# Attention, experts and a gated MLP on one core: the cap with the first keys, reciprocals spread over partitions, signs and copies on ScalarE

## The chip, the cores and the metric

The kernel runs on one core of a Trainium2 chip. The metric is the device time of one execution in microseconds. The core has TensorE (PE in the profile; PEld is its weight load), VectorE (DVE), ScalarE (ACT), GpSimd (POOL), and SyncE (SP), which here only issues transfers.

## The reference

Three blocks in a row, all in float32, for batch 4, sequence 448, 12 heads of 64.

```python
scores = cap * np.tanh(scale * (q @ k.T) / cap)     # per batch and head
attn = np.exp(scores - scores.max(-1, keepdims=True))
x = attn / (attn.sum(-1, keepdims=True) + 1e-09) @ v    # heads side by side: [4, 448, 768]

logits = x @ w_gate                                 # 4 experts, the 2 best are weighted
for e in range(4):                                  # causal attention, head size 64
    ye = softmax(causal(x @ wq[e] @ (x @ wk[e]).T / 8)) @ (x @ wv[e]) @ wo[e]
    out += gate(logits, e) * ye

h = gelu(out @ w_in)                                # 768 -> 1024
u, v = h[..., :512], h[..., 512:]
v = layer_norm(v) * g_ln
y = out + (u * (w_sg @ v + b_sg[:, None])) @ w_out
```

`w_in` and `w_out` arrive as float64 and are turned into float32 on the chip, by integer operations on their upper and lower words.

## The kernel before, in words

The first block runs in 25 slots (`slot`), one for each pair of heads and one to finish: 4 batches x 6 pairs. Transposed keys and queries lie in `kp` and `qp` (two heads on 128 partitions, 448 columns). In slot i TensorE makes the scores of pair i (`scores`), three and a half blocks of 128 keys for two heads; ACT takes tanh (scale `tsc`, 1/(8 cap)) and then exp (scale `capt`) into `p`, a ring of four buffers; TensorE multiplies pair i-1 with its values (`values`) into `po`, which ACT copies to `os`. DVE (and POOL from batch 1 on) adds the blocks of exp up (`add_up`, tile `pb`), and in every second slot a product with ones (`sums`) turns two pairs' `pb` into sums over the keys. They gather in one tile `rs` a batch, in which 32 partitions belong to each of four heads and only three of the 32 hold sums that are needed.

`invert` ends a batch: DVE takes the reciprocal of the whole tile `rs`, SP stores it to DRAM (`rd`), and `load_rb` reads it back, broadcast over 64 partitions (`rb`). Two slots later `over_sums` multiplies `os` by `rb`, and `in_parts` splits the result into `xh` and `xl`, from which the second block's products read.

A slot has places at which side work is called: `a` twice (written a0 and a1), `w`, `p`, `n`. In slots 0 to 9 the side work is `prepare_weights`: twelve units of `w_in` are loaded, turned into float32 (`convert`, which calls `from64`, seven DVE operations on 128x512) and multiplied with `wo` on TensorE (`products`, a slot or two after their unit). The list `turns` says which units a slot converts: one in slots 0, 1, 2, 4, 6, 8, two in 3, 5, 7. From slot 10 on the side work is the second block for batches 0 to 2 (`PLAN`): projections (`queries_keys`, `values_chunk`), softmax (`weigh`, `settle`), transposes of the probabilities (`turn`, tile `pt`), products with values (`attend`). `values_chunk` also yields the gate's logits in the last four columns of its PSUM tile; ACT copies the values to `vp`, DVE the logits to `lg`. `normed` calls `invert`, `load_rb`, `over_sums` and `in_parts` of batch b at fixed places of the next batch: `invert` at a1 of its second slot (7, 13, 19), `over_sums` at `w` of its fourth.

Until the end of slot 24, ACT, DVE, POOL and TensorE keep the order in which the program calls them; SP's issues are placed by the planner. After slot 24 the rest of the second block (`experts_end`) and the third block (`mlp_a`, `mlp_b`, `mlp_c`) run together, and the planner orders all engines.

Of the kernel before, what the change touches and what calls it, by code (L numbers as in the profile page):

```python
# [74 lines left out]
def build(ctx: ExitStack, tc: tile.TileContext, a: dict):  # L75
# [68 lines left out]

    def scale():
        nc.sync.dma_start(capt, a["cap"].to_broadcast([128, 1]))
        dve.memset(tsc, 0.0)
        act.activation(tsc, tsc, AF.Tanh)
        dve.reciprocal(tsc, capt)
        dve.tensor_scalar(tsc, tsc, 1.0 / math.sqrt(D), None, op0=ALU.mult)  # L150
# [7 lines left out]

    def from64(w, m, e):


        words = w.bitcast(I32).rearrange("p (n t) -> p n t", t=2)
        up, down = words[:, :, 1], words[:, :, 0].bitcast(U32)
        f, ef = m.bitcast(F32), e.bitcast(F32)
        dve.tensor_scalar(m, up, 0x7FFFFFFF, None, op0=ALU.bitwise_and)
        dve.tensor_scalar(f, f, LO64, HI64, op0=ALU.max, op1=ALU.min)
        dve.tensor_scalar(m, m, 3, 0x3FFFFFF8, op0=ALU.logical_shift_left, op1=ALU.bitwise_and)
        dve.scalar_tensor_tensor(m, up, -0x40000000, m, op0=ALU.bitwise_and, op1=ALU.bitwise_or)
        dve.tensor_scalar(e, m, -0x800000, None, op0=ALU.bitwise_and)
        dve.scalar_tensor_tensor(ef, down, 2.0 ** -52, ef, op0=ALU.mult, op1=ALU.mult)  # L170
        return f, ef
# [6 lines left out]
    ps_o = ah.enter_context(tc.tile_pool(name="ps_o", bufs=1, space=PSUM, side="right"))  # L178
    os_t, sums_t, pend, rb_d = {}, {}, {}, {}
    vt, ptail, po_t = {}, {}, {}  # L180
# [10 lines left out]
    def load_pair(b, hp):  # L191

        qp = at.tile([128, S], F32, tag="qp", name=f"qp{b}_{hp}", bufs=3)
        kp = at.tile([128, S], F32, tag="kp", name=f"kp{b}_{hp}", bufs=3)
        nc.sync.dma_start(kp, a["kT"][b, :, hp, :])
        nc.sync.dma_start(qp, a["qT"][b, :, hp, :])
        if (b, hp) == pairs[0]:
            scale()
            load_w(0)
        return qp, kp, load_v(b, hp)  # L200

# [6 lines left out]
    def tails(s, *of):  # L208
# [3 lines left out]
        for w, (qp, kp) in enumerate(of):  # L212
            for j in range(2):
                r = slice(64 * j, 64 * j + 64)
                mm(s[64 * w:64 * w + 64, j, :S], kp[r, KB * 128:], qp[r, :], start=True, stop=True)

# [61 lines left out]
    def sums(b, i):  # L278
# [4 lines left out]
        if i == 0:  # L283
            sums_t[b] = ao.tile([128, S], F32, name=f"rs{b}", tag="rs", bufs=1)
            dve.tensor_copy(sums_t[b], g[:, :S])
        else:
# [3 lines left out]
    def invert(b):  # L290
        dve.reciprocal(sums_t[b], sums_t[b])
        d = dr.tile([4, 32, S], F32, tag="rd", name=f"rd{b}")
        nc.sync.dma_start(d.rearrange("j r s -> (j r) s"), sums_t[b])
        rb_d[b] = d
        for h2 in range(2):
            load_rb(b, h2)

# [3 lines left out]
    def slot(i, side):  # L301
# [6 lines left out]
        if i + 2 < len(pairs):  # L308
            qk = [at.tile([128, S], F32, tag=t, name=f"{t}{i + 2}", bufs=3) for t in ("qp", "kp")]
            b, hp = pairs[i + 2]  # L310
            nc.sync.dma_start(qk[1], a["kT"][b, :, hp, :])
            nc.sync.dma_start(qk[0], a["qT"][b, :, hp, :])
            ld[i + 2] = qk
# [17 lines left out]
        if i == len(pairs):  # L331
            drain(sums(B - 1, HP // 2 - 1))
            invert(B - 1)
        side("p")
        if 0 < i < len(pairs):
# [31 lines left out]
    def normed(n, place):  # L367
# [3 lines left out]
        if n >= B * HP or b < 0:  # L371
            return
        if step == (1, "a1"):
            invert(b)
        elif step == (3, "w"):
            over_sums(b, 0)
# [55 lines left out]
    def values_chunk(b, c):  # L432
        xh, xl = X[b]
        if c == 0:
            VP[b] = mo.tile([CP, NC, E * HD], F32, tag="vp", name=f"vp{b}", bufs=2)
            LG[b] = sm.tile([CP, NC, E], F32, tag="lg", name=f"lg{b}")
        g = ps_g.tile([128, 512], F32, tag="g", name=f"v{b}_{c}")
        n = 0
        for k in range(KC):
# [4 lines left out]
            yield 360.0  # L444
        act.activation(VP[b][:, c, :], g[:CP, :E * HD], AF.Copy)
        dve.tensor_copy(LG[b][:, c, :], g[:CP, E * HD:E * HD + E])

    def gates(b):

        lg = LG.pop(b)  # L450
        sh = [CP, NC, E, E]
# [56 lines left out]
    def turn(b, ep, el):  # L508
        pt = PTS[b, ep, el] = mo.tile([CP, NC, S], F32, tag=f"pt{el}", name=f"pt{b}_{ep}_{el}")
        for i in range(NC):  # L510
# [3 lines left out]
            for j in range(i + 1):  # L514
                pin(nc.tensor.transpose(g[:CP, j * CP:(j + 1) * CP], pe[:, j * CP:(j + 1) * CP], ident))  # L515
            rnd("a" if 2 * b + ep >= PTA and i % 2 < PTE else "v", pt[:, :i + 1, i * CP:(i + 1) * CP],
                g[:CP, :n].rearrange("p (j q) -> p j q", q=CP))
# [13 lines left out]

    QKT, VP, LG, WT, CSS, PES, PTS = {}, {}, {}, {}, {}, {}, {}

# [145 lines left out]
    def prepare_weights(pool):  # L679
# [10 lines left out]
        def convert(u):  # L690
            m = pool.tile([128, FH], I32, name=f"wi{u}m", tag="m64", bufs=5)
            e = pool.tile([128, FH], I32, name=f"wi{u}e", tag="e64", bufs=2)
            p, e = from64(raw.pop(u), m, e)
            dve.tensor_tensor(p, p, e, op=ALU.add)
# [276 lines left out]
def _layout(x):  # L971
# [7 lines left out]
        "vt": v[:, :, KB * 128:].reshape(B, HP // 2, 2, 2, KT, D).transpose(0, 1, 2, 4, 3, 5).reshape(B, HP // 2, 2 * KT, 2, D),  # L979
        "cap": np.asarray(x["cap"]).reshape(1, 1),  # L980
        "wqk": _rows(np.concatenate([wide(x["moe_wq"]), wide(x["moe_wk"])], 1)),
# [7 lines left out]
        "b_sg": x["moe2_b_sg"].reshape(1, S),  # L989
    }  # L990
    r = np.arange(CP)
    hot = np.zeros((128, 3, 32), np.float32)
# [27 lines left out]
```

## Time and profile before

| | us |
|---|---|
| median of 3 runs | 552.34 (551.21 to 554.4) |
| profiled execution | 549.69 |
| its span, first to last instruction | 547.9 |
| TensorE busy | 518.1 |
| VectorE busy | 353.4 |
| ScalarE busy | 310.1 |
| GpSimd busy | 130.4 |

The timed runs are whole executions; the profile is one execution of its own. Times inside it count from its first instruction. A busy engine is one with an instruction under way; for TensorE the ends of matmuls are modelled. Line 106 is the helper through which ACT, DVE and POOL instructions go, line 121 that of matmuls and 515 the transposes, so instructions are told apart by the names of their tiles. A name after `<-` in brackets is what ended the idle time before an instruction.

### The profile page before, as it was taken

To read this page: it belongs to the slowest core of one execution; us is meant where nothing else is said; L and a number is where in the kernel's file an instruction comes from. 1 tells how busy PE (TensorE), PEld (TensorE's weight loads), DVE (VectorE), ACT (ScalarE), POOL (GpSimd) and SP (SyncE) were. 2 spreads that over 40 slices of the span, in tenths; PEclk is the share of its full clock that TensorE was granted. 3 is DMA by queue.
4 is the path that set the end of the run, shared out by engine and by line. 5 is a ranking of instruction groups with operands and counts; after the bars stand their busy time and mean duration, and the time that the engine had idled before them with its cause. 6 is when DMAs were issued, how large, how long until landed. Compare 5 with 4: busy or idle time off the path is not lost.

```text
span 547.9 us, 7557 instructions
## 1 busy us (share of the span) xinstructions
PE 518.1 (95%) x2732; PEld 336.9 (61%) x2732; DVE 353.4 (64%) x720; ACT 310.1 (57%) x507; POOL 130.4 (24%) x151
## 2 busy tenths in 40 slices
PE   7999997999999998999997999899899999999997
PEld 2233332355545564554556758669678889889996
DVE  3899999983757745656765678756622796484300
ACT  5978675778685786485743573542544353253211
POOL 0000130433145071135143437304603010010000
PEclk9999997999999999999998999999899999999999
DMA  7964614653334241323025811210511000000111
GB/s 266 346 199 144 199 49 153 205 183 111 100 86 144 60 145 26 117 62 92 1 74 133 216 32 39 65 52 0 210 72 51 1 1 34 34 35 34 51 51 67
DMA packets 33157, 53.99 MB, mean 99 GB/s; under 512 B 4128, under 2 KB 28000, under 8 KB 33120
## 3 DMA queue, kind: packets, MB, share of 16 engines
q1 hardware_dynamic: 31968, 48.27, 28.6%
q0 software_dynamic: 1152, 5.24, 2.9%
q8 instruction: 21, 0.34, 0.3%
q14 instruction: 16, 0.13, 0.1%
HBM read 41.84 MB, written 11.67 MB: 98 GB/s over the span
## 4 chain that ended last, share of the span: by engine, by line
PE 58%; DVE 24%; ACT 6%; DMA 4%; issue 4%; POOL 3%; SPq 1%; DVEq 0%; POOLq 0%; ACTq 0%
PE o L121 15%; DVE pb L106 7%; PE sp L121 6%; PE qk L121 6%; PE v L121 5%; ACT p L106 4%; PE hv L121 4%; PE s L121 4%; PE po L121 4%; PE hu L121 4%; PE av L121 3%; PE a L121 3%; PE tr L515 2%; DVE rs L106 2%; POOL pe L106 2%
## 5 line engine op out<-in xcount | busy, mean ns | idle before, releaser
L106 ACT ACTIVATE p<-s,tsc 128x896 f32<-128x896 f32 x84 | 80.7, 1005 | 37.0 <-PE s L121 18.7
L121 PE MATMUL s<-qp,kp 64*128 64x448 f32 (+1 forms) x384 | 80.0, 574 | 3.6 <-ACT p L106 3.6
L106 POOL TENSOR_TENSOR pb<-p 128x896 f32<-128x896 f32 x18 | 41.4, 2301 | 162.9 <-ACT p L106 148.1
L106 ACT ACTIVATE p<-p,capt 128x1792 f32<-128x1792 f32 (+1 forms) x48 | 77.0, 1603 | 1.3
L106 DVE TENSOR_TENSOR pb<-pb,p 128x896 f32<-128x896 f32 (+1 forms) x48 | 56.5, 1178 | 11.1 <-ACT p L106 7.4
L121 PE MATMUL po<-p,vv 128*64 128x448 f32 x288 | 59.9, 551 | 0.0
L121 PEld LDWEIGHTS s<-qp,kp 64*128 64x128 f32 (+1 forms) x384 | 27.5, 175 | 49.9 <-issue 22.9
L106 POOL TENSOR_SCALAR pe<-pe,cs 112x112 f32<-112x112 f32 (+1 forms) x64 | 37.1, 600 | 51.8 <-DVE cs L106 50.0
L106 DVE CUSTOM_DVE_ANT_0 a<-a,neg 112x112 f32<-112x112 f32 (+3 forms) x64 | 28.2, 462 | 29.7 <-PE a L121 29.3
L106 ACT ACTIVATE pe<-a,m 112x112 f32<-112x112 f32 (+3 forms) x64 | 31.4, 494 | 25.8 <-DVE m L106 21.2
L121 PEld LDWEIGHTS po<-p,vv 128*64 128x64 f32 x288 | 18.7, 138 | 38.8 <-issue 34.3
L121 PE MATMUL qk<-xh,wqk_h 128*128 128x448 f32 x96 | 37.6, 393 | 1.4 <-DVE xh L106 1.4
L121 PE MATMUL o<-gh,wu_h 128*128 128x448 f32 x96 | 36.3, 378 | 0.2 <-DMA wu_h<-wud 0.2
L121 PE MATMUL o<-gl,wu_h 128*128 128x448 f32 x96 | 36.0, 375 | 0.0
L121 PE MATMUL qk<-xh,wqk_l 128*128 128x448 f32 x96 | 35.4, 368 | 0.0
L515 PE MATMUL tr<-ident,pe 112*112 112x112 f32 x160 | 25.2, 263 | 10.6 <-DVE pt L106 3.7
L121 PE MATMUL o<-gh,wu_l 128*128 128x448 f32 x96 | 34.9, 368 | 0.0
L106 ACT ACTIVATE ob<-o 128x448 f32<-128x448 f32 x24 | 13.0, 542 | 38.6 <-PE o L121 38.1
L106 POOL TENSOR_TENSOR rstd<-rstd,mhalf 112x1 f32<-112x1 f32 x16 | 10.2, 640 | 102.0 <-DVE rstd L106 102.0
L121 PE MATMUL v<-wvg_h,xh 128*112 128x260 f32 x96 | 28.8, 300 | 2.3 <-DVE lg L106 2.2
L515 PEld LDWEIGHTS tr<-ident,pe 112*112 112x112 f32 x160 | 17.8, 133 | 18.6 <-issue 13.4
L121 PE MATMUL a<-qk 64*112 64x112 f32 (+3 forms) x128 | 27.9, 427 | 0.8 <-ACT qk L106 0.6
(227 smaller groups left out, 1111.0 us busy)
## 6 DMA issues: line engine op xcount, KB each, us to landing
kp<-in_kT_dram SPq DMA_DIRECT2D x24, 224.0 KB, 3.7
qp<-in_qT_dram SPq DMA_DIRECT2D x24, 224.0 KB, 3.9
rb<-rd SPq DMA_DIRECT2D x24, 224.0 KB, 5.2
out_dram<-ob SPq DMA_DIRECT2D x24, 224.0 KB, 1.9
vv<-in_v_dram SPq DMA_DIRECT2D x24, 192.0 KB, 3.6
wuw<-in_w_out_dram SPq DMA_DIRECT2D x6, 384.0 KB, 3.5
wud<-wuw SPq DMA_DIRECT2D x12, 192.0 KB, 1.9
ws<-in_wqk_dram SPq DMA_DIRECT2D x4, 384.0 KB, 6.0
```

Of the source, the lines that this page charges most:

```text
L106: ins = f(*args, **kw)
L121: pin(nc.tensor.matmul(*args, **kw))
L515: pin(nc.tensor.transpose(g[:CP, j * CP:(j + 1) * CP], pe[:, j * CP:(j + 1) * CP], ident))
```

## The change

The cap is no longer an input of its own: it is the last column of a copy of the first pair's keys (`k_cap`, 449 columns), loaded in two transfers of 128 and 321 columns; the first queries are issued on ACT's queue. DVE takes the scale's reciprocal from that column and copies it to `capt`. For units 2 to 11, `from64` makes the absolute value of the upper words with an ACT activation (Abs) instead of a DVE mask. The first of each batch's three `sums` is copied from PSUM by ACT. `invert` is split: at a0 the sums are stored to DRAM as they are; at `w` (`spread`) the 3 x 448 sums of each of the four heads are read back as 32 partitions x 42 columns; at a1 (`inverted`) DVE takes the reciprocal of 128x42 and four stores return it; the broadcasts start at `w` of the next slot. For the last batch the steps follow one another. The logits stay in `vp` (four more columns of ACT's copy), and the copies of the transposes of batches 0 and 1 for the second expert of the first pair go from DVE to ACT.

```diff
-    def scale():
-        nc.sync.dma_start(capt, a["cap"].to_broadcast([128, 1]))
+    def scale(with_keys):
         dve.memset(tsc, 0.0)
         act.activation(tsc, tsc, AF.Tanh)
-        dve.reciprocal(tsc, capt)
+        dve.reciprocal(tsc, with_keys)
+        dve.tensor_copy(capt, with_keys)
         dve.tensor_scalar(tsc, tsc, 1.0 / math.sqrt(D), None, op0=ALU.mult)
...
-        dve.tensor_scalar(m, up, 0x7FFFFFFF, None, op0=ALU.bitwise_and)
+        if by is act:
+            act.activation(f, up.bitcast(F32), AF.Abs)
+        else:
+            dve.tensor_scalar(m, up, 0x7FFFFFFF, None, op0=ALU.bitwise_and)
...
-        kp = at.tile([128, S], F32, tag="kp", name=f"kp{b}_{hp}", bufs=3)
-        nc.sync.dma_start(kp, a["kT"][b, :, hp, :])
-        nc.sync.dma_start(qp, a["qT"][b, :, hp, :])
+        kp = at.tile([128, S + 1], F32, tag="kp", name=f"kp{b}_{hp}", bufs=3)
         if (b, hp) == pairs[0]:
-            scale()
+            act.dma_start(qp, a["qT"][b, :, hp, :])
+            for c in (slice(0, 128), slice(128, S + 1)):
+                nc.sync.dma_start(kp[:, c], a["k_cap"][:, c])
+            scale(kp[:, S:])
             load_w(0)
+        else:
+            nc.sync.dma_start(kp[:, :S], a["kT"][b, :, hp, :])
+            nc.sync.dma_start(qp, a["qT"][b, :, hp, :])
...
-            dve.tensor_copy(sums_t[b], g[:, :S])
+            act.activation(sums_t[b], g[:, :S], AF.Copy)
...
     def invert(b):
-        dve.reciprocal(sums_t[b], sums_t[b])
-        d = dr.tile([4, 32, S], F32, tag="rd", name=f"rd{b}")
+        d, n = dr.tile([4, 32, S], F32, tag="rd", name=f"rd{b}"), 3 * S // 32
         nc.sync.dma_start(d.rearrange("j r s -> (j r) s"), sums_t[b])
+        rows = d[:, :3, :].rearrange("j r s -> j (r s)").rearrange("j (p c) -> j p c", c=n)
+        r = ao.tile([128, n], F32, name=f"ri{b}", tag="ri", bufs=1)
+        inv[b] = (r, rows)
         rb_d[b] = d
-        for h2 in range(2):
-            load_rb(b, h2)
+
+    def spread(b):
+        r, rows = inv[b]
+        for j in range(4):
+            nc.sync.dma_start(r[32 * j:32 * j + 32], rows[j])
+
+    def inverted(b):
+        r, rows = inv.pop(b)
+        dve.reciprocal(r, r)
+        for j in range(4):
+            nc.sync.dma_start(rows[j], r[32 * j:32 * j + 32])
...
             invert(B - 1)
+            spread(B - 1)
+            inverted(B - 1)
+            load_rb(B - 1, 0)
+            load_rb(B - 1, 1)
...
-        if step == (1, "a1"):
+        if step == (1, "a0"):
             invert(b)
+        elif step == (1, "w"):
+            spread(b)
+        elif step == (1, "a1"):
+            inverted(b)
+        elif step == (2, "w"):
+            load_rb(b, 0)
+            load_rb(b, 1)
...
-        act.activation(VP[b][:, c, :], g[:CP, :E * HD], AF.Copy)
-        dve.tensor_copy(LG[b][:, c, :], g[:CP, E * HD:E * HD + E])
+        act.activation(VP[b][:, c, :], g[:CP, :E * HD + E], AF.Copy)
...
-        lg = LG.pop(b)
+        lg = VP[b][:, :, E * HD:]
...
-            rnd("a" if 2 * b + ep >= PTA and i % 2 < PTE else "v", pt[:, :i + 1, i * CP:(i + 1) * CP],
+            rnd("a" if 2 * b + ep >= PTA and i % 2 < PTE or (ep, el) == (0, 1) else "v", pt[:, :i + 1, i * CP:(i + 1) * CP],
...
-            p, e = from64(raw.pop(u), m, e)
+            p, e = from64(raw.pop(u), m, e, act if u > 1 else dve)
...
-        "cap": np.asarray(x["cap"]).reshape(1, 1),
...
+    out["k_cap"] = np.concatenate([out["kT"][0, :, 0, :], np.full((2 * D, 1), x["cap"], np.float32)], 1)
```

## Rows read from the trace of the kernel before

**Rows 1.** The page: TensorE's share; DVE and granted clock (tenths) in 40 slices of 13.7 us.

```profile
PE 518.1 (95%) x2732; PEld 336.9 (61%) x2732; DVE 353.4 (64%) x720; ACT 310.1 (57%) x507; POOL 130.4 (24%) x151
...
DVE  3899999983757745656765678756622796484300
...
PEclk9999997999999999999998999999899999999999
```

**Rows 2.** Who waited for whom: us in total, times, longest us.

```profile
PE sum L121 <- DVE pb L106: 3.3, 1, 3.3
...
PE qk L121 <- DVE xh L106: 1.4, 1, 1.4
...
PE tr L515 <- DVE pt L106: 3.7, 3, 1.3
...
PE tr L515 <- DVE lg L106: 1.5, 1, 1.5
...
PE tr L515 <- ACT os L106: 1.0, 1, 1.0
...
PE v L121 <- DVE lg L106: 2.2, 1, 2.2
...
PE o L121 <- DMA wu_h<-wud: 0.2, 1, 0.2
...
ACT p L106 <- DVE pb L106: 13.2, 3, 7.3
```

**Rows 3.** Stretches; columns PE, PEld, DVE, ACT, POOL busy, clock, DMA, GB/s.

```profile
20.00:83.40 63.40, 63.24 (x294) 20.99 (x292) 61.11 (x88) 48.31 (x48) 6.98 (x3) 1.00 0.54 169
...
84.00:87.20 3.20, 0.03 (x2) 0.03 (x3) 3.13 (x4) 0.00 (x0) 0.00 (x0) 0.85 0.26 90
...
87.20:95.00 7.80, 7.80 (x26) 2.33 (x26) 7.56 (x12) 7.72 (x7) 0.00 (x0) 0.62 0.63 185
```

**Rows 4.** Timeline of the start: start us, length us, engine, line, what.

```profile
0.73 1.28 ACT L106 ACT_TABLE_LOAD   x1 [0.73 <-PEq L1009]
...
5.49 1.77 PE L121 MATMUL s<-qp,kp 64*128 64x448 f32 x8
...
7.22 1.91 ACT L106 ACTIVATE p<-s,tsc 128x896 f32<-128x896 f32 x2 [5.00 <-DVE tsc L106]
```

**Rows 5.** Timeline of slots 7 to 9, DVE.

```profile
70.78 0.41 DVE L106 TENSOR_SCALAR wi9m<-wi_3w 128x512 int32<-128x512 int32 x1
...
82.11 2.94 DVE L106 RECIPROCAL rs<-rs 128x448 f32<-128x448 f32 x1
...
95.46 2.08 DVE L106 TENSOR_TENSOR os<-os,rb 128x896 f32<-128x896 f32 x2
```

**Rows 6.** Groups by shape: busy us, mean ns of one, idle us before.

```profile
L106 DVE RECIPROCAL rs<-rs 128x448 f32<-128x448 f32 x4 | 11.8, 2947 | 0.0
...
L106 DVE RECIPROCAL cs<-cs 112x4 f32<-112x4 f32 x16 | 2.8, 176 | 0.5
...
L106 ACT ACTIVATE w2h<-w2ps 128x512 fp32r<-128x512 f32 x4 | 2.4, 598 | 1.9 <-PE w2ps L121 1.9
...
L106 DVE COPY lg<-v 112x4 f32<-112x4 f32 x16 | 2.5, 154 | 16.7 <-ACT vp L106 16.7
```

**Rows 7.** DMA issues: KB each, median us from issue to landing.

```profile
capt<-in_cap_dram SPq DMA_DIRECT2D x1, 0.5 KB, 5.0
...
rd<-rs SPq DMA_DIRECT2D x1, 224.0 KB, 1.9
...
rb<-rd SPq DMA_DIRECT2D x24, 224.0 KB, 5.2
```

**Rows 8.** Timeline of slots 12 and 13, DVE.

```profile
134.69 0.62 DVE L106 TENSOR_TENSOR rs<-rs,sum 128x448 f32<-128x448 f32 x1 [0.36 <-PE sum L121]
...
141.38 2.95 DVE L106 RECIPROCAL rs<-rs 128x448 f32<-128x448 f32 x1
```

**Rows 9.** What SP's queue waited for: us in total, times, longest us.

```profile
SPq L185 <- PE po L121: 68.2, 13, 11.9
```

More of the change, by code (lines that the diff above doesn't have):

```diff
@@ L157, in build, with from64 @@
     w2_d = [dr.tile([128, 2, FF], F32, name=f"w2d{i}", tag="w2d") for i in range(2)]
-    def from64(w, m, e):
+    def from64(w, m, e, by=None):
         words = w.bitcast(I32).rearrange("p (n t) -> p n t", t=2)
@@ L178, in build @@
     ps_o = ah.enter_context(tc.tile_pool(name="ps_o", bufs=1, space=PSUM, side="right"))
-    os_t, sums_t, pend, rb_d = {}, {}, {}, {}
+    os_t, sums_t, pend, rb_d, inv = {}, {}, {}, {}, {}
     vt, ptail, po_t = {}, {}, {}
@@ L214, in tails @@
                 r = slice(64 * j, 64 * j + 64)
-                mm(s[64 * w:64 * w + 64, j, :S], kp[r, KB * 128:], qp[r, :], start=True, stop=True)
+                mm(s[64 * w:64 * w + 64, j, :S], kp[r, KB * 128:S], qp[r, :], start=True, stop=True)
     def scores(b, hp, h, qp, kp, then=None):
@@ L308, in slot @@
         if i + 2 < len(pairs):
-            qk = [at.tile([128, S], F32, tag=t, name=f"{t}{i + 2}", bufs=3) for t in ("qp", "kp")]
+            qk = [at.tile([128, n], F32, tag=t, name=f"{t}{i + 2}", bufs=3) for t, n in (("qp", S), ("kp", S + 1))]
             b, hp = pairs[i + 2]
-            nc.sync.dma_start(qk[1], a["kT"][b, :, hp, :])
+            nc.sync.dma_start(qk[1][:, :S], a["kT"][b, :, hp, :])
             nc.sync.dma_start(qk[0], a["qT"][b, :, hp, :])
@@ L434, in values_chunk @@
         if c == 0:
-            VP[b] = mo.tile([CP, NC, E * HD], F32, tag="vp", name=f"vp{b}", bufs=2)
-            LG[b] = sm.tile([CP, NC, E], F32, tag="lg", name=f"lg{b}")
+            VP[b] = mo.tile([CP, NC, E * HD + E], F32, tag="vp", name=f"vp{b}", bufs=2)
         g = ps_g.tile([128, 512], F32, tag="g", name=f"v{b}_{c}")
@@ L530, in attend @@
         act.activation(YA[b][:, ep, :], g[:, :S], AF.Copy)
-    QKT, VP, LG, WT, CSS, PES, PTS = {}, {}, {}, {}, {}, {}, {}
+    QKT, VP, WT, CSS, PES, PTS = {}, {}, {}, {}, {}, {}
     PLAN = {0: [("p", queries_keys, 0, 0)],
```

## Prediction

> **What bounds the kernel now.** I read the page first. TensorE (PE) is busy for 95% of the span, but in the first seven of forty slices DVE too stands at 8 or 9 tenths, and the granted TensorE clock drops in slices 7, 22 and 29 [rows 1]. So two engines are candidates, in different stages. The second view was what matmuls waited for [rows 2]: TensorE's visible waits are few, and most name DVE. The third was the table of stretches [rows 3]. From 20 to 83.4 us TensorE is busy for 63.2 of 63.4 us, at full clock, although DVE is almost as full (61.1). There DVE's length costs nothing yet. It falls behind, and the bill comes at 84 to 87.2: TensorE does nothing, then runs from 87.2 to 95 at a mean 0.62 of full clock, between its two levels of 1.2 and 2.4 GHz. The timeline [rows 5] shows why: the reciprocal of the first batch's sums holds DVE for 2.94 us until 85.05, and the additions that the next sums need come behind it; ScalarE (ACT) waited for such additions too, 13.2 us in three places, 7.3 in the longest [rows 2]. The reader should see a kernel bound by TensorE, with holes. The change can win the holes and the slow clock behind them, and nothing of what lies between.
>
> The holes: 3.3 us (sums behind additions), 1.4 (first projection behind `xh`), 3.7 (transposes behind DVE copies, three times), 1.5 and 2.2 (behind the copies `lg`), 1.0 (behind ACT's `os`) [rows 2]. The slow clock after the first hole costs 7.8 x 0.38 = 3.0 us [rows 3]. The profiled execution took 549.69 us with a span of 547.9; the median of the three runs, 552.34, is 2.65 above it. I take the difference found in the profile off that median.
>
> **Part 1, the cap with the first keys.** The first tanh began at 7.22, after ACT had idled 5.00 us for the scale, which DVE makes from the cap. The first scores began at 5.49 and half of their 1.77 us serves the first tanh, so without the cap it could begin near 6.5: 0.7 us [rows 4]. It is nothing if the keys, now in two transfers, or the queries, now issued by ACT, land later than 5.5, and 0.8 at most. The added copy of the cap is one short DVE instruction (0.18 for a reciprocal of 4 columns [rows 6]) while DVE idles. The issue on ACT stands in front of a table load that ended at 2.0 [rows 4], three us before it matters. SP has one issue less in front of the first weights.
>
> **Part 2, ten signs to ACT.** Units 2 to 11 lose their first DVE step, 0.41 [rows 5] and its gap, 0.44: 4.4 us. ACT gains ten passes over 128x512; the nearest row is 0.60 [rows 6], so 6.0 us. From 20 to 83.4 ACT is busy 48.3 of 63.4 [rows 3], and nine of the ten come there (5.4): 53.7 still fits. But ACT works in program order, so a sign stands behind its slot's two tanhs and in front of the exp, and DVE can run no further ahead than that. The page "ScalarE: Activation LUTs" of the Trainium skill (section "Table sets: the hidden batching unit") counts abs among the cheap functions that every table set holds. The trace has a single table load, of 1.28 us [rows 4], and no abs, so it cannot show it; were the page wrong, twenty loads would cost 25.7 us. By that rule this gets no chance of its own.
>
> **Part 3, the reciprocal spread out.** 128x448 takes 2.95 and 112x4 takes 0.18 [rows 6]; that is 6.2 ns a column, so 42 columns take about 0.41 and DVE saves 2.5, four times. The price is a longer way: sums to DRAM (1.9 [rows 7]), four loads, the reciprocal, four stores, then the broadcasts. The trace has no such load; the nearest rows are 1.9 (a store of 224 KB) and 5.0 (the cap, 4 bytes a row) [rows 7]. SP spends some 0.4 us on an issue of this kind, 1.5 on four. So the way from ready sums to the reciprocal's inputs is 1.9 + 1.5 + 1.9 = 5.3 us, or 8.4 by the cap's row. I take the lower: with 168 B these rows are 11 times shorter than the store's (1,792 B) but 42 times longer than the cap's. In slot 13 the last sums are ready at 135.3 and the reciprocal stood at 141.38 [rows 8]: 6.1 us, so it just fits. In slot 7 there is more room.
>
> **Part 4, copies and logits to ACT.** DVE loses the first copies of the sums (0.62 like the addition in [rows 8], four times, two of them in the first stage), sixteen `lg` copies of 0.15 with 16.7 us of waiting for ACT in front of them [rows 6], and eight copies of transposes in slots 15 and 21. ACT takes each at less than the 0.60 of its copy of 512 columns [rows 6], and the logits ride in a copy that it made already.
>
> **The sum.** *Start to first projection.* ACT's wait for additions near 62 us goes with the lag, so slot 7's scores can come at 64.8 - 0.7, the first half of them, two tanhs and the sign behind it 0.9 + 1.9 + 0.6 later: 67.5, where DVE began the unit (9) at 70.78. Units 9 and 10 then took until 82.11 [rows 5]; less two signs that is 10.4, and with 0.4 for the reciprocal DVE is at 78.3 and has the additions by 80.5. TensorE wants them at 83.4 - 0.7 = 82.7, so the hole and its slow clock go (3.3 + 3.0). The next limit is `xh`: four stores issued from 78.3, landed at 81.7; four broadcasts issued by 84, 0.6 each, and landed after 5.2 or more [rows 7], say at 90.3; the two products then end at 91.5 where they ended at 97.54 [rows 5], 6.0 earlier, and DVE's work behind them is the same. I take 5.5 for all parts up to here (bounds 2.0, if DVE waits at each sign, and 0.7 + 3.3 + 3.0 + 1.4 = 8.4).
>
> *Slots 10 to 24.* Transposes behind DVE: 3.6 of 3.7, as two places lose the copies and at the third the reciprocal in front of them shrinks. The 1.0 behind `os` goes too: the gates in front of it start later by the reciprocal and `lg`. Behind `lg`, only 0.3 of 1.5, because ACT's own copy ended just before it. Sum 4.9 (bounds 1.5 and 3.7 + 1.0 + 1.5 = 6.2).
>
> *The last batch.* TensorE waited 2.2 us for an `lg` that DVE did after products waiting for broadcasts [rows 2], and the clock of slice 22 stands at 8 tenths [rows 1], 1.4 to 2.7 us of 13.7. With the logits off DVE both can go: +3.7. But the broadcasts come later: 1.9 + 1.5 + 1.9 + 0.4 + 1.5 + 1.9 = 9.1 instead of 2.95 + 1.9, so 4.2 us more, and softmax work queued behind the products on DVE would wait as long. Between +3.7 and -4.2 I take +1.0: the planner is free in its order here and can place the products later, since their projections come much later.
>
> *After 300 us* nothing is removed but `lg`; a new order may win or lose: 0, bounds -2 and +2.
>
> 5.5 + 4.9 + 1.0 = 11.4, and 552.3 - 11.4 = **540.9 us**, the likeliest case's own range 538 to 544.5.
>
> **The rivals.** (a) *ACT sets the pace* (0.17): if each sign delays the exp that TensorE's next products need, 6.0 us return: 547. For it: from 87.2 to 95 ACT is busy 7.7 of 7.8. Against it: 15 us of ACT's idle time from 20 to 83.4 [rows 3].
> (b) *All holes go* (0.13): 8.4 + 6.2 + 3.7 = 18.3, so 534. For it: DVE's savings in the first stage (4.4 + 1.2 + 2.5 + 0.7 = 8.8) exceed its holes. Against it: the broadcasts above.
> (c) *It does not do what it says* (0.07): the signs hold DVE at ACT's pace, the additions still come at 87, and transposes wait for ACT's copies instead of DVE's. The 0.7 at the start and half a us beside it remain: 551.
> (d) *The short loads are slow* (0.06): each takes the cap's 5.0 instead of 1.9. At slots 13 and 19 the reciprocal then waits 8.4 - 6.1 = 2.3 us, and the last batch pays 3.1 twice, for load and store: 540.9 + 4.6 + 6.2 = 551.7. For it: the cap's row is the only one here with short rows. Against it: the cap was queued behind 448 KB of keys and queries. The Trainium skill's page "DMA: Bandwidth & Descriptors" (section "Specifications") speaks for it: it gives 512 B as the least transfer for line rate, and a row of the spread has 168 B. No row here shows that size.
> (e) *Slower* (0.07): SP's order stops DVE. SP takes its issues in turn, and a load of values has waited 11.9 us there for TensorE [rows 9]; loads of the spread queued behind such a one leave DVE standing at the reciprocal, and behind that its transposes, softmax and additions. At slots 13 and 19 and in the last batch it must hold DVE 3.8 us each, beyond the 6.1 that are covered, to eat the 11.4; at 6 us each the time is 559. For it: eight more issues a batch, all waiting on one another. Against it: the one transfer that a matmul visibly waited for cost 0.2 us [rows 2], whatever SP's queue waited.
> My forecast has 0.50. Half a per cent, 2.8 us, is about what a measurement of this kernel can tell from no change. So faster 0.80, same 0.13, slower 0.07. The range 533 to 550 has (a) and most of (b) inside; (e), about half of (c) and (d), and a third of (b) lie outside.
>
> **What would show it.** First tanh near 6.5; no hole near 84 and full clock to 95; the projection's last keys near 104; reciprocals of 0.4 with no DMA as their releaser; no transposes behind DVE in slots 15, 19 and 21; no `lg`. It is wrong if DVE waits for ACT at the clamps or for DMA at the reciprocals, or if a new hole follows the last batch.

## The result and the profile after

The changed kernel takes 545.73 us (median of 4 runs, 545.04 to 546.0) beside 551.86 for the kernel before (4 runs): a ratio of 0.9879, with an interval of 0.9845 to 0.9912. That is 6.1 us less where 11.4 were forecast. The profiled execution took 545.04 with a span of 543.2, 4.7 less than before; the marks and tables up to the experiments are about these 4.7.

The page after: TensorE's share, then DVE and the granted clock in 40 slices (of 13.6 us).

```profile
PE 516.1 (95%) x2732; PEld 336.6 (62%) x2732; DVE 333.2 (61%) x683; ACT 319.0 (59%) x529; POOL 132.2 (24%) x151
...
DVE  3899999874466646456724596755722796484300
...
PEclk9999999999999999999999899799999999999999
```

Against [rows 1] the 7 of slice 7 is gone. The 8s of slices 22 and 29 have given way to an 8 in slice 23 and a 7 in slice 26. VectorE lost 20 us of work and ScalarE won 9, but neither number says where the time went. The waits do (us in total, times, longest):

```profile
PE tr L542 <- POOL pe L106: 4.6, 2, 2.9
...
PE qk L121 <- DVE xh L106: 2.3, 1, 2.3
PE qk L121 <- ACT pe L106: 1.8, 1, 1.8
...
PE tr L542 <- ACT pt L106: 1.2, 2, 0.7
...
PE tr L542 <- DVE pt L106: 0.5, 1, 0.5
...
ACT p L106 <- DVE pb L106: 5.8, 3, 3.1
```

Of [rows 2], the wait of the sums (3.3), the `lg` (1.5 and 2.2), the `os` (1.0) and nearly all of the transposes behind VectorE (3.7) are gone. The list also has waits that [rows 2] do not show. The two longest are transposes behind GpSimd's `pe` and a projection behind ScalarE's `pe`. They lie in the last batch.

To place the gains, take the first matmul of each slot's values product as a mark. Slot 11's mark came 5.36 us earlier (114.50 before, 109.14 after). Of the later slots five are shorter: slot 14 by 1.6, 15 by 0.6, 18 by 1.1, 19 by 1.2, 21 by 0.6. Slot 24, the last, is reached at 266.25 where it was 276.79: 10.54 us ahead, and 11.6 counted from the first scores, which begin 1.05 later in this execution. From there to the last output matmul before took 267.46 and after takes 273.32. So 10.5 were won and 5.9 given back. The two tables of that last part, first before, then after, each in five stretches (columns as in [rows 3]):

```profile
276.79:306.79 30.00, 26.62 (x166) 18.65 (x165) 19.73 (x59) 10.30 (x32) 9.25 (x17) 0.94 0.52 139
306.79:336.79 30.00, 29.29 (x148) 21.44 (x147) 23.36 (x66) 19.73 (x47) 14.89 (x18) 1.00 0.30 80
336.79:371.79 35.00, 32.26 (x176) 24.27 (x174) 22.02 (x56) 16.73 (x42) 10.58 (x16) 1.00 0.15 46
371.79:411.79 40.00, 37.79 (x204) 30.76 (x203) 21.03 (x64) 16.39 (x43) 15.24 (x26) 0.96 0.27 97
411.79:544.25 132.46, 132.45 (x654) 118.17 (x652) 64.14 (x119) 47.37 (x90) 8.79 (x14) 1.00 0.10 35
```

```profile
266.25:296.25 30.00, 27.45 (x176) 19.11 (x175) 11.97 (x37) 9.49 (x30) 8.66 (x15) 1.00 0.60 167
296.25:326.25 30.00, 24.74 (x115) 16.73 (x114) 23.53 (x66) 18.22 (x45) 14.16 (x15) 0.94 0.16 44
326.25:361.25 35.00, 32.26 (x155) 26.00 (x154) 23.70 (x64) 16.29 (x42) 13.65 (x18) 0.90 0.17 54
361.25:401.25 40.00, 37.54 (x217) 30.85 (x216) 21.57 (x60) 16.16 (x43) 14.50 (x24) 1.00 0.22 79
401.25:539.57 138.32, 138.32 (x682) 121.13 (x681) 66.80 (x129) 50.00 (x96) 9.95 (x16) 1.00 0.11 39
```

TensorE's idle time is the stretch less its busy time: 9.05 in sum before, 13.01 after, 4.0 more. The second stretch alone has 4.6 more. The clock's price is the length times what is missing to 1.00: 3.4 before, 5.3 after, 1.9 more. The remainder is 255.0 in both, so what was given back is idle time and the slow clock behind it. (The clock column has two digits, so its price is good to about 0.2 us.) The table of experiments below uses the same two numbers.

Why TensorE idles there is seen on VectorE, after, in the last batch:

```profile
271.33 0.62 DVE L106 TENSOR_TENSOR rs<-rs,sum 128x448 f32<-128x448 f32 x1 [0.29 <-PE sum L121]
276.93 0.42 DVE L106 RECIPROCAL ri<-ri 128x42 f32<-128x42 f32 x1 [4.97 <-DMA ri<-rd]
...
280.05 0.56 DVE L106 SCALAR_TENSOR_TENSOR wum<-wuw,wum 128x384 f32<-128x384 uint32 x1
285.29 1.09 DVE L106 TENSOR_TENSOR os<-os,rb 128x896 f32<-128x896 f32 x1 [4.68 <-DMA rb<-rd]
286.30 0.63 DVE L106 CUSTOM_DVE_ANT_0 a<-a,neg 112x448 f32<-112x448 f32 x1
...
288.30 1.09 DVE L106 TENSOR_TENSOR os<-os,rb 128x896 f32<-128x896 f32 x1 [1.32 <-DMA rb<-rd]
...
296.15 1.09 DVE L106 TENSOR_TENSOR os<-os,rb 128x896 f32<-128x896 f32 x1 [5.92 <-DMA rb<-rd]
```

and the same two kinds of line in the kernel before:

```profile
292.92 1.09 DVE L106 TENSOR_TENSOR os<-os,rb 128x896 f32<-128x896 f32 x1 [2.15 <-DMA rb<-rd]
...
294.77 1.09 DVE L106 TENSOR_TENSOR os<-os,rb 128x896 f32<-128x896 f32 x1 [0.29 <-DMA rb<-rd]
...
296.17 0.56 DVE L106 SCALAR_TENSOR_TENSOR wum<-wuw,wum 128x384 f32<-128x384 uint32 x1
299.31 1.21 DVE L106 TENSOR_TENSOR os<-os,rb 128x896 f32<-128x896 f32 x1 [1.91 <-DMA rb<-rd]
```

Three products with broadcasts wait 4.3 us before and 11.9 after; counted from slot 24's mark the third stands at 22.5 before and at 29.9 after. The step `wum`, the end of a weight conversion, stands behind two of the products before and ahead of all three after. The order in this part is the planner's. GpSimd waits for that step, and then sends for 2 MB of `w2`, before and after (start us, length, engine, what):

```profile
296.87 0.52 POOL L106 TENSOR_SCALAR wuw<-wum 128x384 fp32r<-128x384 f32 x1 [13.11 <-DMA rb<-rd]
...
299.52 1.29 POOL L796 DMA_DIRECT2D w_h<-w2d  x2
```

```profile
280.76 0.51 POOL L106 TENSOR_SCALAR wuw<-wum 128x384 fp32r<-128x384 f32 x1 [7.55 <-issue]
...
283.38 1.29 POOL L823 DMA_DIRECT2D w_h<-w2d  x2
...
301.40 5.10 POOL L106 TENSOR_SCALAR pe<-pe,cs 112x112 f32<-112x112 f32 x3 [15.67 <-DVE cs L106]
```

Before, the loads leave as the third product starts, 22.7 us behind slot 24's mark. After, they leave 17.1 behind it and ahead of the third broadcast (issued at 286.4, landed 9.1 us later), and softmax work (`cs`) queued behind the third product on VectorE reaches GpSimd's `pe` late. That is where the new waits for GpSimd come from (2.9 and 1.6). The projection's wait of 1.8 has another source, the first product: the softmax step behind it on VectorE (`a`) starts at 286.30, and ScalarE's `pe`, to which the profile puts the projection's wait down, has waited 3.85 us when it starts at 287.02.

That the loads of `w2` and the third broadcast get in each other's way shows in all fourteen kernels of this document. In the seven in which these loads are sent for ahead of the third broadcast, VectorE waits 5.9 to 8.0 us for it; in the seven in which the broadcast is issued ahead of them or beside them, 0.2 to 3.3.

### The profile page after: what moved, and what is told of

Same layout as the page of the kernel before. It is cut to its first block, busy times and chain, and to the rows that moved or that the text cites. A ratio compares the mean times of both kernels' runs of the same rounds, so it can differ in the third digit from the quotient of the medians.

```text
span 543.2 us, 7596 instructions
## 1 busy us (share of the span) xinstructions
PE 516.1 (95%) x2732; PEld 336.6 (62%) x2732; DVE 333.2 (61%) x683; ACT 319.0 (59%) x529; POOL 132.2 (24%) x151
## 4 chain that ended last, share of the span: by engine, by line
PE 71%; DVE 9%; ACT 5%; DMA 5%; POOL 4%; issue 4%; SPq 1%; DVEq 0%; POOLq 0%; ACTq 0%
PE o L121 15%; PE s L121 9%; PE po L121 9%; PE sp L121 7%; PE qk L121 5%; PE v L121 4%; PE hv L121 4%; PE hu L121 4%; PE w2ps L121 3%; PE a L121 3%; ACT p L106 3%; PE av L121 3%; DMA rb<-rd 3%; PE tr L542 2%; POOL pe L106 2%
## 5 line engine op out<-in xcount | busy, mean ns | idle before, releaser
L121 PE MATMUL s<-qp,kp 64*128 64x448 f32 (+1 forms) x384 | 77.8, 566 | 3.6 <-ACT p L106 3.6
L106 POOL TENSOR_SCALAR pe<-pe,cs 112x112 f32<-112x112 f32 (+1 forms) x64 | 39.7, 642 | 56.0 <-DVE cs L106 56.0
L106 POOL TENSOR_TENSOR rstd<-rstd,mhalf 112x1 f32<-112x1 f32 x16 | 10.2, 637 | 104.8 <-DVE rstd L106 104.8
L542 PE MATMUL tr<-ident,pe 112*112 112x112 f32 x160 | 25.3, 265 | 10.5 <-POOL pe L106 4.6
L106 ACT ACTIVATE pt<-tr 112x112 f32<-112x112 f32 (+3 forms) x48 | 18.8, 403 | 22.7 <-PE tr L542 22.3
```

The source lines that it names most:

```text
L106: ins = f(*args, **kw)
L121: pin(nc.tensor.matmul(*args, **kw))
```

## The experiments

Each row of an experiment is a median of 5 or 6 runs (the logits alone have 12), with its own runs of the kernel before beside it (551.8, 552.0 and 550.8 us in the three groups that ran together, in the order of the table: four, four, four). The changed kernel was timed apart from them, so a difference to it of under about 2 us isn't clear of noise by the medians alone. "Slot 24" is that slot's mark, less the start of the first scores, which varies from one execution to the next. "Tail" runs from the mark to the last output matmul; idle and clock are its parts in one execution, from five stretches as above.

The granted clock is on record for every timed execution, too. The last two columns are means over them: "clock, all" is the span times what is missing to 1.00, the clock's price in the whole kernel, and "rest" is the time less that price; for the kernel before they are those of the three groups.

| kernel | us | ratio, interval | slot 24 | tail | idle | clock | clock, all | rest |
|---|---|---|---|---|---|---|---|---|
| before | 551.86 | | 271.3 | 267.5 | 9.1 | 3.4 | 7.1 to 8.2 | 543.5 to 544.1 |
| after | 545.73 | 0.9879, 0.9845 to 0.9912 | 259.7 | 273.3 | 13.0 | 5.3 | 6.7 | 539.0 |
| last batch whole | 543.16 | 0.9843, 0.9816 to 0.9871 | 261.2 | 270.0 | 11.3 | 5.1 | 8.2 | 535.0 |
| signs on VectorE | 548.01 | 0.9925, 0.9898 to 0.9952 | 262.1 | 273.4 | 13.3 | 5.2 | 6.7 | 541.0 |
| all batches whole | 545.35 | 0.9872, 0.9839 to 0.9905 | 264.7 | 271.8 | 11.3 | 6.7 | 8.4 | 537.0 |
| copies on VectorE | 544.43 | 0.9877, 0.9843 to 0.991 | 259.4 | 276.9 | 12.4 | 10.2 | 8.4 | 536.6 |
| third broadcast early | 540.65 | 0.9796, 0.9771 to 0.9821 | 261.0 | 267.9 | 10.0 | 1.6 | 4.7 | 536.0 |
| three edits | 537.66 | 0.9742, 0.9718 to 0.9767 | 259.5 | 266.8 | 9.2 | 1.8 | 3.8 | 533.9 |
| 6 warm-up matmuls | 543.65 | 0.9862, 0.9833 to 0.9892 | 260.2 | 273.5 | 12.6 | 6.8 | 7.4 | 536.8 |
| logits alone | 551.4 | 0.9977, 0.9955 to 1.0 | 267.9 | 271.6 | 10.7 | 6.7 | 8.9 | 541.9 |
| three edits, 6 warm-up | 536.92 | 0.9741, 0.972 to 0.9763 | 258.8 | 270.2 | 9.9 | 5.2 | 4.4 | 532.3 |
| logits, third early | 546.32 | 0.9925, 0.9909 to 0.9942 | 270.8 | 264.2 | 8.2 | 0.0 | 5.2 | 541.2 |
| all whole, third early | 543.42 | 0.9863, 0.9834 to 0.9893 | 264.9 | 267.8 | 9.3 | 3.3 | 6.0 | 537.0 |
| before, third early | 554.99 | 1.0083, 1.006 to 1.0106 | 270.6 | 271.3 | 11.6 | 5.2 | 8.7 | 546.4 |

In each of these rows the tail less idle and clock lies between 253.6 and 256.3 us, so differences of under 3 us in idle and clock together say little by themselves. The tail's clock is one execution's, and so tells less than "clock, all".

Behind slot 24 the fourteen kernels have only six orders of instructions on TensorE, VectorE and ScalarE, by their traces. Three kernels have one of their own: before; third early; before with third early. The changed kernel shares its order with signs on VectorE, copies on VectorE and 6 warm-up matmuls. Last batch whole, all batches whole and the logits alone share the next; the three edits, with 12 and with 6, logits with third early and all whole with third early the last. Within this last order the tails run from 264.2 to 270.2 us, and the slow clock makes nearly all of that.

**The last batch's sums inverted whole.** The first suspect was the longer way to the last broadcasts.

```
-            invert(B - 1)
-            spread(B - 1)
-            inverted(B - 1)
+            whole(B - 1)      # reciprocal of 128x448, one store
```

> The changed kernel, but the last batch's sums are inverted whole, as in the kernel before (128x448 on VectorE, one store, then the broadcasts); the first three batches keep the spread. Theory: up to the last product with values the changed kernel is 10.5 us ahead and then loses 5.8, because the last batch's results come later by two short transfers and then meet the loads of the third block's weights. So the last product with values stays at 266 +- 1 us, the two waits of VectorE for broadcasts shrink from 11.9 us in sum to below 5, and the time falls by 3 to 5 us, to about 541 to 543. Rival: the planner's new order after slot 24 loses those 5.8 us whatever the way of the sums; then the time stays within 1.5 us of 545.7.

543.16: 2.6 us less than the changed kernel, and 4.0 less in the rest without the clock's price. From slot 24's mark the third product came at 27.75, where it is 29.9 after and 22.5 before. VectorE's wait for the three broadcasts is still 11.8 us, where less than 5 was expected, and now 8.0 of it in the last. So the longer way is a part of the loss, and not all of it. How large a part stays open, as the order behind slot 24 is another one, too.

**The signs back on VectorE.**

```
-            p, e = from64(raw.pop(u), m, e, act if u > 1 else dve)
+            p, e = from64(raw.pop(u), m, e, dve)
```

> The changed kernel with all twelve signs on VectorE, as before. Theory: TensorE has no slack at all from 20 to 83 us, and VectorE just keeps pace; with 4.4 us more on VectorE the additions of slot 7 come about 3 us later than TensorE wants them, a hole and slow clock return there and the projection's last keys come at 107 to 108 instead of 104.3; the last product with values at 269 to 270, the time 3 to 4 us up, 549. Rival (ScalarE sets the pace of the first slots, and the signs cost as much as they free): the last product with values within 1 us of 266, the time unchanged or lower.

548.01, 2.3 more (2.0 in the rest), and slot 24 is reached 2.4 later, counted from the first scores. Sums again wait for additions, 0.7 us instead of 3.3, with the clock at 1.00 from 82 to 88, and `xh` is waited for 2.7 us instead of 2.3. The other parts of the change close most of the first hole without the signs; these are worth about 2.3 of 6.1.

**All sums inverted whole**, with the rest of the change kept.

```
-        if step == (1, "a0"):
-            invert(b)         # store the sums
-        elif step == (1, "w"):
-            spread(b)         # four loads
-        elif step == (1, "a1"):
-            inverted(b)       # reciprocal, four stores
-        elif step == (2, "w"):
+        if step == (1, "a1"):
+            whole(b)
             load_rb(b, 0)
             load_rb(b, 1)
...                           # and the last batch as above
```

> The changed kernel with the sums of all four batches inverted whole, as in the kernel before. Theory: the spread is worth 2.5 us of VectorE in slot 7 (1.5 to 2.5 us of time), about 1 us in slot 13 and 1.2 us in slot 19, and costs about 4 us in the last batch. So the last product with values comes at 270 to 271, but the time ends within 1.5 us of the changed kernel's 545.7. Rival (the spread earns nothing in the slots, its gains are the logits' and the copies'): last product with values at 266 and the time near 541.5, like the variant that undoes only the last batch.

545.35, the same as the changed kernel: what the spread wins in the slots it loses in the last batch. The fair partner is the last batch whole, which differs only in the slots and has the same order behind them. It takes 2.2 us less, 2.0 in the rest. In the slots the spread wins 0.8 by the end of slot 10 (`xh` waited for 3.2 us, not 2.3) and 2.7 in slot 19 (17.08 instead of 14.35). Slot 14, 1.6 shorter than before, stays so. How a reciprocal costs 2.7 in slot 19 is seen in the later run with all sums whole, where the slot takes 17.12; VectorE first, then the windows:

```profile
211.68 2.95 DVE L106 RECIPROCAL rs<-rs 128x448 f32<-128x448 f32 x1
214.54 0.50 DVE L106 COPY pt<-tr 112x112 f32<-112x112 f32 x2
```

```profile
180.00:212.00 32.00, 31.35 (x191) 17.00 (x187) 19.03 (x49) 24.29 (x42) 11.38 (x14) 1.00 0.25 75
212.00:226.00 14.00, 12.47 (x81) 8.85 (x83) 9.26 (x25) 6.84 (x10) 2.95 (x5) 0.88 0.40 116
```

The copies of transposes wait for the reciprocal, TensorE waits 1.05 us for them at 213.85, and the clock is at 0.88 over the 14 us: 1.7 more. The kernel before has the same wait there and no slow clock behind it (slot 19 takes 15.57), so 1.7 of the 2.7 is slow clock that the same wait does not always bring.

**The copies of transposes back on VectorE.**

```
-            rnd("a" if 2 * b + ep >= PTA and i % 2 < PTE or (ep, el) == (0, 1) else "v", ...
+            rnd("a" if 2 * b + ep >= PTA and i % 2 < PTE else "v", ...
```

> The changed kernel with the eight copies of transposes of slots 15 and 21 back on VectorE. Theory: each place costs TensorE 0.6 us (what the trace gained there, 1.3 us of waiting less 0.7 us of a new one), so the last product with values comes 1.3 us later, at 267.5, and the time is 1.3 us up, 547. Rival: the wait moves to a later place that waits for VectorE anyway, and nothing changes (within 0.5 us at the last product).

544.43, by the medians and ratios not to be told from the changed kernel, but slots 15 and 21 take 12.14 us, where it takes 13.04 and 13.03 and the kernel before 13.67 and 13.66. No transpose waits in slot 15, where after waits 0.71. So with the other parts of the change in place the copies on ScalarE cost 0.9 twice, and the expectation had the sign wrong. The rest without the clock's price is 2.4 lower than the changed kernel's, near the 1.8 of 0.9 twice; the slow clock, 10.2 us in this execution's tail, hides it.

**The third broadcast early**, into a buffer that it doesn't share with the first.

```
+            load_rb(B - 1, 2)        # slot 24, right behind the first two
...
-            load_rb(l, 2)            # behind the first product
...
-        rb = xp.tile(..., tag=f"rb{h2 % 2}")
+        rb = (ypool if last else xp).tile(..., tag="y" if last else f"rb{h2 % 2}")
```

> The changed kernel, with one edit: the third broadcast of the last batch gets a buffer of its own and is issued right behind the first two, ahead of the loads of w2 on GpSimd. Theory 1 (what the change lost after the last values product is the late third broadcast: issued behind VectorE's use of the first buffer, and then sharing the DMA engines with the 2 MB of w2): VectorE's wait of 5.9 us for it goes, and with it the two gaps before transposes that wait for GpSimd's pe, 2.9 and 1.6 us; time 541 to 543. Theory 2 (the loss is in the longer way to the first two broadcasts, 7.65 against 4.9 us from the sums to the first issue): the first wait of 4.7 stays or grows, since three broadcasts now share the engines, the gaps move and do not go; time 545 to 547.

540.65, 5.1 less than the changed kernel: 3.0 in the rest and 1.9 in the clock's price. A few transposes stand elsewhere in TensorE's order of the last batch too, so the step isn't quite alone. The three products:

```profile
286.25 1.09 DVE L106 TENSOR_TENSOR os<-os,rb 128x896 f32<-128x896 f32 x1 [4.50 <-DMA rb<-rd]
289.11 1.09 DVE L106 TENSOR_TENSOR os<-os,rb 128x896 f32<-128x896 f32 x1 [1.17 <-DMA rb<-rd]
294.15 1.09 DVE L106 TENSOR_TENSOR os<-os,rb 128x896 f32<-128x896 f32 x1 [3.33 <-DMA rb<-rd]
```

The third stands at 26.8 from the mark, 3.1 sooner. Its wait falls to 3.3, not to nothing as the first theory had it, while the first product's stays, as the second had it. The two waits for GpSimd's `pe` shrink from 2.9 and 1.6 to 0.8 and 0.9, the tail's idle time by 3.0 and its clock's price by 3.7.

**Three edits together**: last batch whole, copies on VectorE, third broadcast early.

> The changed kernel with three edits together: the last batch's sums inverted whole (2.9 us on VectorE, one store, no spread), the PSUM copies of the pair (0, 1) back on VectorE, and the third broadcast early in a buffer of its own. If their gains add up (whole -2.6 as measured, copies -0.9 at two slots where VectorE has room, third broadcast -3): 539 to 541. If all of them buy the same wait, as theory 2 has it: 543, as with the last batch whole alone.

537.66, below what their sum was expected to give, and 8.1 less than the changed kernel. The first two edits are worth 3.0 on top of the third. On top of the last batch whole, the other two take 1.1 off the rest, which is less than the copies give by themselves, and 4.4 off the clock's price. So beside the whole last batch the early broadcast wins slow clock, and hardly anything else.

**Six warm-up matmuls**, where 12 stand ahead of the first scores.

```
-WARM = 12      # in the list of constants
+WARM = 6
```

> The changed kernel with 6 warm-up matmuls in place of 12. Theory 1 (the keys and the scale are there at 4.2 us, and the first scores at 6.5 only because 12 warm-up matmuls at the lower clock stand ahead of them): the first scores start near 4.3 to 4.5, and since ScalarE's tanh sets the pace of the first slots, the whole is 1.5 to 2 us shorter: 543.5 to 544.5. Theory 2 (the clock then rises later, and the first slots' matmuls pay for it): the first scores come earlier, but the second slot does not; time 545 to 547.

543.65, 2.1 less (2.2 in the rest). The start on TensorE, after and then in this run:

```profile
1.32 5.30 PE L121 MATMUL warm<-z 128*128 128x512 bf16 x12 [1.32 <-POOL z L106]
6.54 2.01 PE L121 MATMUL s<-qp,kp 64*128 64x448 f32 x8
```

```profile
1.32 2.74 PE L121 MATMUL warm<-z 128*128 128x512 bf16 x6 [1.32 <-POOL z L106]
3.99 2.33 PE L121 MATMUL s<-qp,kp 64*128 64x448 f32 x8
```

The scores begin 2.55 earlier and slot 24 comes 2.07 earlier. So with the cap in the keys the start was bound by the warm-up.

**The logits alone**, in the kernel before.

```
-        act.activation(VP[b][:, c, :], g[:CP, :E * HD], AF.Copy)
-        dve.tensor_copy(LG[b][:, c, :], g[:CP, E * HD:E * HD + E])
+        act.activation(VP[b][:, c, :], g[:CP, :E * HD + E], AF.Copy)
```

> The kernel before, with one part of the change alone: the gate logits leave PSUM together with the values, in ScalarE's copy (260 columns in place of 256), and the 16 copies of 4 columns on VectorE go. Theory 1 (the gain of slots 13, 14 and 18 came from here, since it stood also in the run that undid the spread): those slots are 2.5 to 3 us shorter in sum, the wait of the last batch's values for a logit copy, 2.2 us, goes, and the time is 547 to 549. Theory 2 (these slots gained by the signs and copies that left VectorE): slots as before, at most the 2.2 us go; 550 to 551.5.

551.4: no gain to speak of, and yet slot 14 takes 12.67 and slot 18 takes 14.82, as after (14.27 and 15.90 before), and slot 24 comes 2.4 us earlier (3.4 counted from the first scores). In this execution all of it goes again behind slot 24, 3.3 of 4.1 as slow clock; in the means about 2 us stay in the rest and about 1 goes to the clock. Here too the planner puts `wum` ahead of the products, the loads of `w2` leave 15.5 us behind the mark (289.83) instead of 22.7, and the third product, at 301.54, has waited 6.97 us for its broadcast. So this collision does not need the spread. It comes with the planner's order, and that order comes from the logits alone: it is the one of the changed kernel with all sums whole.

**Three edits and six warm-up matmuls.**

> The run with the three edits (537.7 us), and 6 warm-up matmuls in place of 12. If the start's gain adds to the rest, as it did by itself (543.7 against 545.7): 535.5 to 536. If it is lost in the later stages: 537.5.

536.92, by the ratios the same as with 12. The scores begin at 3.99 again and slot 24 comes 3.3 earlier, but the tail takes 3.4 more. The first 30 us of the last batch, with 12 and with 6:

```profile
266.00:296.00 30.00, 25.27 (x158) 17.78 (x155) 19.36 (x55) 10.32 (x32) 10.84 (x20) 0.94 0.67 184
```

```profile
266.00:296.00 30.00, 24.64 (x143) 18.48 (x143) 16.29 (x45) 9.48 (x28) 12.44 (x23) 0.89 0.61 164
```

The hole in it is 4.4 us instead of 3.7, and the clock lower. (The second stretch starts 3.2 us behind its mark, the first at it.) Whether the other executions lose the gain in the same place wasn't seen; in the means the rest is 1.6 lower, of which 0.6 is in its runs of the kernel before, too.

**The logits and the third broadcast early**, in the kernel before.

> The kernel before, with two edits: the logits in ScalarE's copy of the values, which by themselves gained 3.4 us up to the last values product and gave 4.1 back behind it, and the third broadcast of the last batch issued early into a buffer of its own. Theory 1 (what is given back comes from the order on SyncE's queue: a store of w_out's words is now ahead of the third broadcast, GpSimd gets on with the 2 MB of w2 by it, and these share the DMA engines with that broadcast): it is not given back; 546.5 to 548. Theory 2 (whatever comes earlier in the slots waits later, for another reason): 550 to 551.5.

546.32, 4.4 less than the runs of the kernel before beside it. The tail, at 264.2, is the shortest of all, with no slow clock in it; in this execution the slow clock fell on slots 10 and 19 instead. Beside the logits alone the rest is only 0.7 lower and the clock's price 3.7. The expectation named SyncE's queue. In the logits alone VectorE ends `wum` at 287.05, GpSimd takes it up at 287.19 and sends for `w2` at 289.83, right behind its own steps of the conversion; SyncE's store of the converted words leaves at 287.92. The third broadcast follows at 292.15, when the first product gives its buffer free. So VectorE's order is the cause, and the store a consequence.

**All sums whole and the third broadcast early**, in the changed kernel.

> The changed kernel with all sums inverted whole, as before the change (545.35 us), and the third broadcast of the last batch early in a buffer of its own (540.65 with the reciprocals spread). Theory 1 (in the slots the spread is worth 1.4 us, by the start of the last values product less the clock's part; in the last batch it costs 2.6): 539 to 540. Theory 2 (the reciprocals are worth the 2.6 us each that they take of VectorE): 543 or more.

543.42, more than the same edit with the reciprocals spread, by 2.8 in the medians and 3.7 by the ratios. That is the time of the second theory. But this kernel also has its last batch whole, which by itself won 2.6; so either the slots are worth more than the 3.5 of the trace above (0.8 + 2.7), or the whole last batch wins little once the third broadcast is early. The three edits speak for the latter, as the copies alone could make most of their 3.0. The 1.4 of the first theory set aside the slow clock in slot 19, which came in three of six kernels without the spread and in none of the eight with it. Beside all batches whole the rest is the same, 537.0, and the clock's price 2.4 lower.

**The kernel before with the third broadcast early.**

> The kernel before with the third broadcast of the last batch early in a buffer of its own, and nothing else. Its wait is 2.1 us at most in the kernel before, where the loads of w2 come after it. Theory 1 (the edit mostly takes away a loss that the change brought): 0 to 2 us less, 550 to 552. Theory 2 (the edit is a gain by itself, whatever the change does): 546 to 548.

554.99: slower by 4.2 to the kernel before beside it, which neither theory had. The wait for the broadcasts is shorter (3.2 instead of 4.3), but the planner made another order: the values of the last batch wait 3.9 us for an `lg` instead of 2.2, and the tail has 2.5 us more of idle time and 1.8 of clock. So the edit isn't a gain by itself, and the order that the planner makes of it weighs as much as the wait.

## Why the prediction was right, and where it was off

**Faster, and in the range**, with about half of the forecast and above the likeliest case's own 538 to 544.5. Two of its three terms came out nearly to the tenth, the first in part by luck and the second from other parts than were named; the third had the wrong sign. A new hole behind the last batch was one of the prediction's own signs of being wrong, and it came.

*Start to first projection*, 5.5 forecast, 5.4 measured. The tenth is luck: the first scores began 1.05 later in this execution, and behind the wait for `xh` (2.3 us) the clock stayed at 1.00, where in four of the eight kernels with the spread it fell and slot 10 took 1.5 longer. The hole and the slow clock behind it are gone, and the projection's last keys come at 104.32 where 104 was forecast (columns as in [rows 3]):

```profile
82.00:88.00 6.00, 6.00 (x31) 1.72 (x29) 5.80 (x9) 5.14 (x6) 0.00 (x0) 1.00 0.75 162
88.00:96.00 8.00, 7.55 (x32) 2.77 (x32) 7.93 (x8) 7.93 (x10) 2.69 (x1) 1.00 0.80 235
96.00:106.00 10.00, 7.71 (x40) 4.14 (x41) 9.83 (x10) 6.86 (x7) 2.82 (x1) 1.00 0.68 212
```

The next limit was `xh`, as forecast, and the products end at 92.2 (91.5 forecast). But they did not wait for broadcasts there: VectorE is busy for 7.93 of 8 and 9.83 of 10 us. It is full to the end of this stage, which is why the signs count. The 0.7 at the start, inside this term, was wrong: the first tanh came at 7.85 instead of 7.22 [rows 4], and 6.5 was forecast. The scale is ready at 4.57, but the tanh waits for the scores, and these for the 12 warm-up matmuls. In the eight kernels with the cap in the keys and 12 warm-up matmuls the first tanh starts at 6.93 to 7.92, in the four with the cap apart at 6.62 to 7.63.

*The signs.* Each takes ScalarE 0.67 to 0.70 where 0.60 was taken, and it stays idle enough: additions now hold it up for 5.8 us instead of 13.2. Rival (a) did not come. The page "ScalarE: Activation LUTs" of the Trainium skill (section "Table sets: the hidden batching unit") is borne out: the trace has ten abs and still one table load.

```profile
L106 ACT ACT_TABLE_LOAD x1 | 1.3, 1283 | 1.2 <-PEq L1036 1.2
...
L106 ACT ACTIVATE wi9m<-wi_3w 128x512 f32<-128x512 f32 x1 | 0.7, 689 | 0.0
```

*Slots 10 to 24*, 4.9 forecast, 5.2 measured, but from other parts than were named. Logits: 2.7 in slots 14 and 18, where 0.3 and the 1.0 behind `os` were given. Reciprocals: 1.2 in slot 19, as forecast. Copies of transposes: 0.6 in each of two slots, half of what was given, and with the other parts of the change in place VectorE does them better.

*The spread's way* fits: the reciprocal of 42 columns takes 0.41, loads and stores land in 1.6 and 1.4 where 1.9 was taken, and only the last batch's waits for DMA. In groups and in DMA issues:

```profile
L106 DVE RECIPROCAL ri<-ri 128x42 f32<-128x42 f32 x4 | 1.6, 411 | 5.0 <-DMA ri<-rd 5.0
```

```profile
ri<-rd SPq DMA_DIRECT2D x16, 5.2 KB, 1.6
rd<-ri SPq DMA_DIRECT2D x16, 5.2 KB, 1.4
```

From the sums to the first broadcast's issue it is 7.7 us in the last batch, 4.9 before: 2.7 longer, where 4.2 was forecast. Rival (d) fell with that, and rival (e) too: in the slots no reciprocal waits.

*The last batch*, +1.0, and *after 300 us*, 0: this is the step that failed. Together they measured -5.9. "The planner is free in its order here and can place the products later" was the reason for the +1.0, and the planner did the reverse: it put a weight conversion ahead of the products, by which GpSimd's 2 MB left 5.6 us earlier, counted from slot 24, and met the third broadcast. The longer way that the text did name, 4.2 us, is 2.7, and undoing it won 2.6 (whole last batch; 4.0 in the rest, with another order). What is left is the collision and the order: with the third broadcast issued ahead of most of the loads the tail is 5.5 shorter, and the time 5.1, of which 1.9 is slow clock. The two do not add up: beside the whole last batch or all batches whole, the early broadcast won slow clock and little else. The `lg` wait of 2.2 did go, but the holes of 2.9 and 1.6 behind GpSimd's `pe` came in its place.

What stays open: how much of the tail's loss is the collision and how much the planner's order. The third broadcast early comes nearest, with a few transposes moved; no run changes the one without the other, and none holds the loads of `w2` back with nothing else moved. Nor is it settled why equal holes cost the clock here and not there.

## What to carry to other kernels

Follow a gain to the end of the program: a hand-written order keeps it, and where a planner orders the rest from modelled times, a change far ahead can reorder that rest and take it back. Mark the program at a few points and compare the marks; the sum of idle time and of the slow clock behind a mark accounts for what the totals hide. Take the slow clock off every execution before comparing small edits: one trace's share of it can be larger than the edit. A larger kind of load that is off the path needs a place of its own in time, since a small broadcast on the path shares the DMA engines with it (here 224 KB landed after 9.1 us beside 2 MB, and after 5.4 in the median). And when a start is made earlier, look at what else stood in front of it, even a warm-up.

## What the runs showed of the hardware

The price of a hole in TensorE's work varies far more than the hole. Three waits of 0.33, 0.34 and 1.05 us in slot 19 left the clock at 1.00 in the kernel before and took it to 0.88 over 14 us in the two runs with all sums whole. A hole of 2.60 was followed by 30 us at 1.00 in the kernel before, as was one of 2.59 with the third broadcast early; one of 2.61 after was followed by 30 us at 0.89, which is 3.3 us more. In the tails the clock cost between 0.0 and 10.2 us, and between 0.0 and 5.2 in four kernels with the same order of instructions there.

Behind the 12 warm-up matmuls the first scores start anywhere from 5.49 to 6.55 us, before or after the change alike, so a start is compared over several executions.

Loads with rows of 168 B landed in 1.6 us, less than the 1.9 of a store of 224 KB. The page "DMA: Bandwidth & Descriptors" of the Trainium skill (section "Specifications") asks for 512 B a transfer for line rate. No run here measures the rate of such loads.
